# Attention kernel's decay table: lam loaded to one partition and broadcast by matmuls, in place of a broadcast load

## The chip, the cores and the metric

One core of one Trainium2 chip. Times are device microseconds (us) of one execution. A difference of over 2% counts as faster or slower. Every ratio here is of executions in the fast state, with a granted TensorE clock of 0.997 to 1.0.

## The reference, cut to what matters

A linear attention with a decay per head feeds a two-layer network. The decay `lam` is 8 numbers; the kernel needs powers of it for each position.

```python
Dmask   = np.where(rel >= 0, lam[:, None, None] ** rel[None], 0.0)   # rel = i - j in a block
lam_pow = lam[:, None, None] ** (pos + 1)
kv_state = lam ** block * kv_state + einsum(kb * lam ** (block - 1 - pos), vb)
...
h = x @ w_in; g = smelu(h); out = g @ w_out        # 3072 x 512, 512 x 2048, 2048 x 512
```

## The kernel before: the parts that matter

The powers are tables: exp(position * ln lam). They need ln lam on all 128 partitions, so lam was loaded with a broadcast source: 128 rows of the same 32 bytes.

```python
lam_b = const.tile([128, H], F32)
nc.scalar.dma_start(out=lam_b, in_=lam.partition_broadcast(128))
...                                              # GpSimd: identity, iota, masks
NKB, NUB, NV = 3 if len(PF) < 2 else 0, 3, 4
...
for t in vi[:2] + kbd[:2] + ubd[:1]:
    nc.vector.memset(t, 0.0)
for t in vi[2:]:
    nc.gpsimd.memset(t, 0.0)                     # two memsets of 128 x 1024 bf16
pos = const.tile([128, 2, NCB], F32)
nc.scalar.copy(pos, pos_i)
for t in kbd[2:] + ubd[1:]:
    nc.vector.memset(t, 0.0)
ln_lam = const.tile([128, H], F32)
nc.scalar.activation(out=ln_lam, in_=lam_b, func=AF.Ln)
arg = const.tile([128, 2, NCB, H], F32)
nc.vector.tensor_tensor(arg..., _bc(pos...), _bc(ln_lam...), op=AX.mult)
nc.scalar.activation(out=tab_q..., in_=arg[:, 1], func=AF.Exp)      # then tab_p, tab_k
...
def cast(c, eng):          # ks = k * table, on VectorE or GpSimd
    eng.tensor_tensor(ks[c], qkv_ld[c, 1], _bc(tab, 2, D), op=AX.mult)
def cast_q(m, e, eng):     # qs = q * table, on VectorE or GpSimd
    eng.tensor_tensor(qs[m, e], qkv_ld[m, 0][:, :, e], _bc(tab_q..., 2, D), op=AX.mult)
def f_m(c, g):             # sc = scores (PSUM) * causal mask, on VectorE
    nc.vector.tensor_tensor(sc_sb[c][:, g], pst[c, g], _bc(causal, 1, HP), op=AX.mult)
def f_g(...):              # the activation: t, then w, then gT, bf16 in SBUF, on VectorE
```

All instructions are put in an order by a plan at build time; the loads of q, k and v go out on one queue (SP), the weights on GpSimd's. In the profile x0f is q, raw and x1f are k, x2f is v; qs and ks are the products; pt and py are PSUM tiles of the transposes that follow.

## Time and profile before

| | before |
|---|---|
| median of the first 6 runs | 220.57 us (219.85 to 220.69) |
| span of the profiled run | 219.9 us; that run took 221.62 us, 1 us above the median |
| TensorE busy | 203.2 us |
| lam landed, tables ready (tab_q) | 6.30, 7.10 us |
| q, raw k landed | 7.2, 9.0 us |
| first transpose on TensorE | 8.92 us |

The lines behind this stand in the prediction, which was made when three of the six runs were known (median 220.63). The way to read it: a head in which TensorE has nothing to do, then a body in which it is busy.

### The profile page before, as it was taken

The page shows a single profiled execution, that of the slowest core. Times are in us where ns is not written, and L with a number is a line of the kernel's source. Part 1 is how long each engine was busy: PE and PEld are TensorE (multiplying, and loading weights), DVE is VectorE, ACT ScalarE, POOL GpSimd, SP SyncE. Part 2 cuts the span into 40 slices and gives each one's busy share as a digit, 9 for nine tenths or more (in the row PEclk, how much of TensorE's full clock was granted, in tenths as well). Part 3 has the DMA queues.
Part 4 walks back from the last instruction along what each step waited for, and adds up shares of the span by engine and source line. Part 5 has one row for each costly group of instructions (what it writes and reads, how often), then busy time and mean ns, then how long its engine had stood idle before and what let it go on. Part 6 is the DMA issues. An engine that isn't in the chain of part 4 may idle for free.

```text
span 219.9 us, 4453 instructions
## 1 busy us (share of the span) xinstructions
PE 203.2 (92%) x1776; PEld 132.5 (60%) x1800; DVE 139.4 (63%) x216; ACT 123.0 (56%) x220; POOL 63.0 (29%) x71
## 2 busy tenths in 40 slices
PE   0299899999999999999999999999999999999994
PEld 0267778685847977777767676744545444444443
DVE  6285678779553798977855967740697655554301
ACT  2247678455737757486747667545765535445030
POOL 8563085208515162804412700432100000000000
PEclk9999999999999999999999999999999999999999
DMA  3999999999998998989999727989785211110122
GB/s 90 282 218 211 177 244 209 186 205 239 159 224 151 226 184 199 187 162 236 204 244 203 152 43 152 201 196 217 250 141 172 50 45 51 48 48 0 51 95 95
DMA packets 96116, 35.42 MB, mean 161 GB/s; under 512 B 78560, under 2 KB 93152, under 8 KB 96096
## 3 DMA queue, kind: packets, MB, share of 16 engines
q1 hardware_dynamic: 91728, 30.94, 65.6%
q0 software_dynamic: 4224, 4.19, 11.9%
q8 instruction: 14, 0.23, 0.5%
q14 instruction: 6, 0.05, 0.1%
q10 hardware_dynamic: 144, 0.00, 0.0%
HBM read 27.27 MB, written 6.29 MB: 153 GB/s over the span
## 4 chain that ended last, share of the span: by engine, by line
PE 88%; DVE 3%; DMA 2%; ACT 2%; issue 2%; POOL 1%
PE ph L470 38%; PE py L518 35%; DMA lam_b<-in_lam_dram 2%; PE ps L398 2%; PE po L428 2%; PE pu L369 2%; PE py L512 1%; DVE sc L410 1%; PE py L332 1%; PE pt L325 1%; PE po L420 1%; PE po L425 1%; PE pu L365 1%; PE po L446 1%; ACT xT L458 1%
## 5 line engine op out<-in xcount | busy, mean ns | idle before, releaser
L470 PE MATMUL ph<-xT,w_in_sb 128*128 128x256 bf16 (+2 forms) x763 | 95.7, 272 | 1.7 <-ACT xT L458 1.2
L479 ACT ACTIVATE r<-ph,one 128x512 bf16<-128x512 f32 x96 | 65.9, 688 | 48.7 <-PE ph L470 32.0
L518 PE MATMUL py<-w_out_sb,gT 128*128 128x512 bf16 x349 | 86.5, 379 | 1.2 <-issue 0.3
L470 PEld LDWEIGHTS <-w_in_sb 128*128 128x128 bf16 x768 | 63.3, 98 | 24.8 <-issue 1.9
L518 PEld LDWEIGHTS <-gT 128*128 128x128 bf16 x368 | 34.8, 98 | 34.8
L489 DVE TENSOR_SCALAR t<-r 128x1024 bf16<-128x1024 bf16 x48 | 25.1, 524 | 37.0 <-ACT r L479 36.9
L500 DVE TENSOR_TENSOR gT<-w,t 128x1024 bf16<-128x1024 bf16 x48 | 39.6, 826 | 1.5
L495 DVE TENSOR_TENSOR w<-r,t 128x1024 bf16<-128x1024 bf16 x48 | 36.7, 765 | 1.5
L287 POOL TENSOR_TENSOR ks<-x1f,tab_k 128x512 bf16<-128x512 f32 x20 | 23.9, 1199 | 31.4 <-DMA x1f<-in_k_dram 16.5
L523 ACT COPY osb<-py 128x512 f32<-128x512 f32 x23 | 13.5, 586 | 17.9 <-PE py L518 16.6
L296 POOL TENSOR_TENSOR qs<-x0f,tab_q 128x512 bf16<-128x512 f32 x15 | 17.5, 1184 | 19.1 <-DMA x0f<-in_q_dram 12.1
L373 ACT CAST ubd<-pu 64x256 bf16<-64x256 f32 x40 | 14.6, 365 | 6.8 <-PE pu L369 3.7
L294 POOL TENSOR_TENSOR qs<-x0f,tab_qn 128x512 bf16<-128x512 f32 x8 | 9.1, 1134 | 27.7 <-DMA x0f<-in_q_dram 18.7
L410 DVE TENSOR_TENSOR sc<-ps,causal 128x512 bf16<-128x512 f32 x12 | 8.3, 689 | 9.8 <-PE pt L398 9.7
L458 ACT CAST xT<-po 128x512 bf16<-128x512 f32 x15 | 8.8, 585 | 8.2 <-PE po L428 5.0
L332 PE MATMUL py<-ident,qs 128*128 128x128 bf16 x16 | 2.4, 306 | 9.6 <-POOL qs L296 8.9
L428 PE MATMUL po<-sc,vi 128*128 128x128 bf16 x112 | 10.5, 219 | 0.0
L428 PEld LDWEIGHTS <-vi 128*128 128x128 bf16 x112 | 8.4, 98 | 1.0
L410 DVE TENSOR_TENSOR sc<-ps,causal_n 128x512 bf16<-128x512 f32 x8 | 5.5, 689 | 5.2 <-PE pt L398 5.2
L425 PE MATMUL po<-qT,ubd 128*128 128x128 bf16 x48 | 8.7, 219 | 0.0
L320 ACT CAST vi<-x2f 128x512 bf16<-128x512 f32 x14 | 8.5, 615 | 0.1
L332 PEld LDWEIGHTS <-qs 128*128 128x128 bf16 x24 | 2.1, 121 | 10.5 <-POOL qs L296 8.9
(84 smaller groups left out, 137.4 us busy)
## 6 DMA issues: line engine op xcount, KB each, us to landing
out_dram<-osb SPq DMA_DIRECT2D x23, 256.0 KB, 2.7
x1f<-in_k_dram SPq DMA_DIRECT2D x22, 256.0 KB, 4.8
x2f<-in_v_dram SPq DMA_DIRECT2D x22, 256.0 KB, 4.8
x0f<-in_q_dram SPq DMA_DIRECT2D x8, 512.0 KB, 5.3
w_in_sb<-in_moe_w_in_dram POOLq DMA_DIRECT2D x4, 512.0 KB, 8.2
w_out_sb<-in_moe_w_out_dram POOLq DMA_DIRECT2D x4, 512.0 KB, 8.5
x0f<-in_q_dram SPq DMA_DIRECT2D x8, 256.0 KB, 4.1
raw<-in_k_dram SPq DMA_DIRECT2D x1, 512.0 KB, 7.7
```

Of the source, the lines that this page charges most:

```text
L287: eng.tensor_tensor(ks[c], qkv_ld[c, 1], _bc(tab, 2, D), op=AX.mult)
L296: eng.tensor_tensor(qs[m, e], qkv_ld[m, 0][:, :, e], _bc(tab_q[:, e, m % (NCB // 2), :], 2, D), op=AX.mult)
L373: nc.scalar.copy(out=ubd[c % NUB][HD[hi], :, HD[hi]], in_=pu[0][HD[hi], :, HD[hi]])
L410: nc.vector.tensor_tensor(sc_sb[c][:, g], pst[c, g], _bc(causal if c < DX else causal_n, 1, HP), op=AX.mult)
L428: nc.tensor.matmul(po[:, hp], lhsT=vi[c % NV][:, hp, hi].rearrange("p a d -> p (a d)"), rhs=sc_sb[c][:, hi, hp, :], start=(cb == 0 and hi ...
L470: nc.tensor.matmul(ph[:, j * m:(j + 1) * m], lhsT=w_in_sb[:, ko, (ni + j) * 128:(ni + j + 1) * 128], rhs=xT[s][:, ko, tok], start=(ko == 0 ...
L479: nc.scalar.activation(out=o, in_=x, func=AF.Relu, bias=one[:, 0:1])
L489: nc.vector.tensor_scalar(t, r, 0.5, 1.0, op0=AX.mult, op1=AX.min)
L495: nc.vector.tensor_tensor(w, r, t, op=AX.subtract)
L500: nc.vector.tensor_tensor(gT[s][:, f - RW * n:f, tok].rearrange("p (a b) m -> p a b m", a=RW), w.rearrange("p a (b m) -> p a b m", m=m), t ...
L518: nc.tensor.matmul(py_t[s, ms], lhsT=gT[s][:, ko, ms * 128:(ms + 1) * 128], rhs=w_out_sb[:, ko, :], start=(ko == 0), stop=(ko == FO - 1))
L523: nc.scalar.copy(out=osb[s, ms], in_=py_t[s, ms])
```

## The change

The intent: load lam as one small row, so that it lands early; make the logarithm there; spread it to 128 partitions with a matmul against a row of ones. A bf16 matmul would round the logarithm, so it is split into three bf16 pieces that add up to it. One buffer less is set to zero, and a constant of the plan is smaller.

```diff
-    lam_b = const.tile([128, H], F32)
-    nc.scalar.dma_start(out=lam_b, in_=lam.partition_broadcast(128))
+    lam_r = const.tile([1, H], F32)
+    nc.scalar.dma_start(out=lam_r, in_=lam.rearrange("(o h) -> o h", o=1))
...
-    NKB, NUB, NV = 3 if len(PF) < 2 else 0, 3, 4
+    NKB, NUB, NV = 2, 3, 4
...
+    ones = const.tile([1, 128], BF16)
+    nc.vector.memset(ones, 1.0)
-    for t in vi[:2] + kbd[:2] + ubd[:1]:
+    for t in vi[:2] + kbd + ubd:
         nc.vector.memset(t, 0.0)
...
-    for t in kbd[2:] + ubd[1:]:
-        nc.vector.memset(t, 0.0)
-    ln_lam = const.tile([128, H], F32)
-    nc.scalar.activation(out=ln_lam, in_=lam_b, func=AF.Ln)
+    rest = const.tile([1, 3, H], F32)
+    nc.scalar.activation(out=rest[:, 0], in_=lam_r, func=AF.Ln)
+    piece = const.tile([1, 3, H], BF16)
+    for i in range(3):
+        nc.vector.tensor_copy(piece[:, i], rest[:, i])
+        if i < 2:
+            nc.vector.tensor_tensor(rest[:, i + 1], rest[:, i], piece[:, i], op=AX.subtract)
+    ln_ps = pp_s.tile([128, HP, 128], F32, name="ps", tag="ps")
+    ln_lam = ln_ps[:, 0, :H]
+    for i in range(3):
+        nc.tensor.matmul(ln_lam, lhsT=ones, rhs=piece[:, i], start=(i == 0), stop=(i == 2))
...
-    FIRST_BYTE = 2950
+    FIRST_BYTE = 2450
```

## The prediction

> **What bounds the kernel now.** I read the page first: the shares of the engines and the span in slices.
>
> ```profile
> span 219.9 us, 4453 instructions
> PE 203.2 (92%) x1776; PEld 132.5 (60%) x1800; DVE 139.4 (63%) x216; ACT 123.0 (56%) x220; POOL 63.0 (29%) x71
> ...
> PE   0299899999999999999999999999999999999994
> ```
>
> TensorE is busy for 203.2 of 219.9 us, and the 16.7 us in which it isn't lie almost wholly at the two ends. The view of busy time in stretches (columns: stretch, its length, then busy us and instructions of PE, weight loads, DVE, ACT, POOL; granted clock, DMA share, GB/s) says where:
>
> ```profile
> 0.00:9.00 9.00, 0.08 (x1) 0.08 (x2) 4.25 (x11) 2.19 (x6) 6.04 (x18) 1.00 0.69 175
> 9.00:21.00 12.00, 10.44 (x129) 8.21 (x130) 6.90 (x14) 7.08 (x15) 7.02 (x7) 1.00 1.17 218
> 21.00:40.00 19.00, 17.55 (x175) 14.84 (x176) 14.33 (x20) 13.93 (x26) 8.48 (x10) 1.00 1.15 206
> 40.00:60.00 20.00, 19.74 (x230) 14.56 (x232) 15.63 (x23) 11.18 (x19) 8.41 (x8) 1.00 1.04 197
> ```
>
> TensorE idles for 8.92 us before its first instruction, 1.56 us between 9 and 21 us, 1.45 us between 21 and 40 us, and from 40 us on about 0.2 us in each 20 us. So the kernel is a head of 8.92 us followed by a TensorE-bound body, with 3.2 us of tail after 216 us. Whatever shortens the head should arrive at the end nearly whole, as long as the body keeps its work and its order. Then I read the chain that ended last, in order of time, for 0 to 9 us (start, duration, what):
>
> ```profile
> 0.83 5.47 DMA lam_b<-in_lam_dram
> 6.30 0.02 issue
> 6.32 0.22 ACT ln_lam L144
> 6.54 0.02 issue
> 6.57 0.27 DVE arg L146
> 6.84 0.02 issue
> 6.86 0.24 ACT tab_q L149
> 7.10 0.13 ACT tab_p L151
> 7.23 0.09 issue
> 7.32 1.56 POOL qs L296
> 8.88 0.05 issue
> 8.92 0.29 PE py L332
> ```
>
> The load of the 8 numbers of lam takes 5.47 us, and three table steps (ln_lam, arg, tab_q) take 0.8 us after it. It looks as if all of this could go. It can't: the product qs also needs q. The list of DMA issues, cut to the one issue at 0.81 us, gives its time to landing:
>
> ```profile
> x0f<-in_q_dram SPq DMA_DIRECT2D x1, 512.0 KB, 6.4
> ```
>
> So q lands at 0.81 + 6.4 = 7.2 us, 0.1 us after tab_q is ready (6.86 + 0.24 = 7.10) and level with tab_p. The chain names the tables, but q is level with them. **This is the main fact of the case**: faster tables by themselves win some 0.1 us. The gain is what q, and k after it, land earlier.
>
> Does removing the wide lam load make q earlier? The DMA view for 3 to 4 us and for 6 to 7 us (q10 carries lam, q1 the loads):
>
> ```profile
> DMA packets 250, 0.10 MB, mean 97 GB/s; under 512 B 65, under 2 KB 250, under 8 KB 250
> q10 hardware_dynamic: 65, 0.00, 3.2%
> ```
>
> ```profile
> DMA packets 684, 0.35 MB, mean 345 GB/s; under 512 B 10, under 2 KB 684, under 8 KB 684
> ```
>
> By stretches of 1 us from 2 us on the rates are 133, 97, 134, 284 and 345 GB/s, and q10 has 3, 65, 49, 27 and no packets. The rate is lowest where lam's packets are densest, and it is full as soon as they are over. That is a coincidence in time, not yet a cause.
>
> **What the Trainium skill says.** "DMA: Bandwidth & Descriptors", section "Queues, rings and completion order": each of the 16 DMA engines takes turns between the queues for which it has work. Lam's packets lie among q's from 3 to 6 us in this trace, which agrees. Same page, "Why a DMA increments its semaphore by 16 and not by 1": a transfer has landed when the last of its engines has posted. The profile page counts 144 packets on q10, which is 128 rows and 16 posts, so lam waits for the slowest of 16 rings. "VectorE: DVE Perf Modes", section "The TRN2 errata": an fp32 tensor_tensor takes (N+151)/0.96 ns. For N = 96 that is 257 ns; the trace has 0.26 us for arg. "TensorE: Matmul & The Clock Gate", section "Single matmul latency": (398+N)/2.4 ns. For N = 128 that is 219 ns; the trace has 219 ns for L428.
>
> **The change part by part.**
>
> 1. Lam to one partition. It removes 127 of 128 row packets and at least 8 of the 16 posts. Its issue stays at 0.83 us. In the trace lam's first packets come at about 3 us (3 of them in 2 to 3 us), since they come behind the first of q's; a transfer with one row, or a few, needs the first of these and a post, so I estimate its landing at 3.4 to 4.2 us, middle 3.8, in place of 6.30.
>
> 2. Set-up on DVE. Before, its memsets run from 0.88 to 4.49 us: 2 of vi in 1.03, 2 of kbd in 1.02, one kbd in 0.48, three ubd in 0.82. One kbd goes (-0.48), a ones row comes (0.06 as for the other small one). DVE is free at about 4.1 us, which is when the logarithm arrives (3.8 + 0.02 + 0.22 = 4.04). Nothing of it is on the path now, as DVE waits 2.08 us for the logarithm. It would be just level with it in the new order.
>
> 3. The splitting. Five dependent DVE operations on 1 x 8 elements: three casts, two subtractions. By the skill's formula a subtraction is (8+151)/0.96 = 166 ns; I take the same for a cast. Between dependent operations of DVE the timeline shows some 0.03 us (t at 24.07 lasts 0.43, w follows at 24.53). Five times 0.166 and four times 0.03 make 0.95 us: 4.1 to 5.05.
>
> 4. Three matmuls of 8 columns with one row. The first two hide under the splitting. The last is (398+8)/2.4 = 169 ns, with two hops of 0.03 us: 0.23 us, to 5.28. Eight columns of TensorE time while it is idle cost nothing.
>
> 5. The tables. arg reads PSUM now: 0.27 to 0.30 us; tab_q 0.24, hops 0.04: ready at about 5.85, tab_p at 5.98. Before: 7.10 and 7.23. So the logarithm costs 1.2 us more than before (0.95 + 0.23), and lam's landing gives 2.5: 1.25 us net.
>
> 6. q. It is 1024 packets of 512 B. By the same view q1 had moved 11 packets by 2 us, and then 260, 185, 263 and 563 in the next four stretches of 1 us, so the 1024th went at about 5.5 us, and q's landing at 7.2 lags that by 1.65 us (the slowest engine, and the receipt). Without the dip I let the fourth and fifth us have 260 to 350 and 350 to 560 packets: the 1024th then goes at about 4.7 to 5.2, and q lands at 6.3 to 6.9. The diff has an opinion of its own: the first-byte constant of the scheduling plan goes from 2950 to 2450 ns, so its writer saw or guessed loads that come 0.5 us earlier: 6.7. I take 6.45. So q, not the tables, ends the head: qs starts at about 6.52 in place of 7.32, 0.8 us earlier.
>
> 7. k and v. The next products wait for them too: DVE's ks waited 1.11 us, to 9.07, for raw k (1.32 + 7.7 = 9.02). The transposes that need it run at 10.58, after ks ends at 9.76: 0.8 us of slack. They come off the same queue as q, so they should move by about as much as q.
>
> The sum: 0.8 us off the head, all of which I count at the end but for 0.07 us, since TensorE is busy for over 98% from 40 us on. 220.63 - 0.73 = **219.9 us**, 0.3%. Even if the whole of lam's wait were won, from 6.30 to 3.8, it would be 2.5 us or 1.1%: the change cannot reach 2% by its mechanism.
>
> **Rivals.** (a) *q is bound by something other than lam*: packets of the first load come slowly for their own reason (descriptors of the first transfers being made), and lam's are only spread by that. For it: before lam's first packet, in 2 to 3 us, the rate is only 133 GB/s, and lam's own packets fill 3.2% of the engines' time. Then q lands at 7.1 to 7.2, nothing is won but the 0.1 us: 220.4 to 220.7. (b) *The lam load was the whole brake*: q lands at 5.3 to 5.8, the tables become the bound at 5.98, qs starts at 6.1: 1.2 us, 219.4; with k and v earlier also some of the 1.56 us of idle time between 9 and 21 us, 218.9. (c) *The plan changes order*: the new constant moves the plan's landing times, and the list order of every engine follows from them. A small inversion in the head (a cast before a table, a transpose before its product) costs or wins 0.3 to 1 us; over the body TensorE's idle time of 0.2 us in 20 us leaves little to win, but a worse order could lose some 1 to 2 us. 218.6 to 221.5. (d) *The one-row chain is much slower than counted*, by 0.3 us per small step: tables at 7.5, slower by 0.3 us: 220.9.
>
> **Range and chances.** I give (a) 0.25, my sum 0.4, (b) 0.25, (d) 0.1, and let (c) widen each by about 0.6 us to both sides; repeats of the kernel before span 0.67 us. The range is 218.7 to 220.9. Faster by over 2% needs 216.2, which no rival reaches but a lucky order: 0.02. Slower by over 2% needs 225.0, an order that breaks the body: 0.02. Within 2%: 0.96.
>
> **What would show it right or wrong.** q10 with a few packets; lam landing at 3.4 to 4.2; DVE's five small operations between 4.1 and 5.1; tab_q ready at about 5.9; qs released by the load of q and not by a table, at 6.3 to 6.9; raw k landed at 8.1 to 8.6; the first matmul of qs at about 8.1 in place of 8.92; 1 us bins from 3 to 5 us at 200 GB/s or more. Wrong: q landing at 7.2 with the same dip in the rate (then (a)), tables after q (then (d)), or a head shorter by 0.8 us whose gain is lost after 21 us (then (c)).

## The result, and the profile after

Ratios here are the mean time of one kernel's fast runs over that of the other's fast runs of the same rounds, so not quite the ratio of the medians quoted.

| | before | after |
|---|---|---|
| median of 6 runs | 220.57 us | 221.83 us (221.33 to 222.58) |
| ratio, 95% interval | | 1.0066 (1.0041 to 1.0091) |
| span of the profiled run | 219.9 us | 220.9 us (222.58 us, the slowest of the six) |
| lam's packets (q10) | 144 | 2 |
| tab_q ready | 7.10 us | 7.00 us |
| q, raw k landed | 7.2, 9.0 us | 5.1, 6.9 us |
| first transpose | 8.92 us | 8.69 us |

The kernel became slower by 0.66%, within the 2% band but outside the stated range: a miss. The order of the instructions, first. Compared row by row on each engine, the two kernels differ only in the set-up that the diff writes; on SP and GpSimd not one row differs, and a build of the changed kernel with the old constant 2950 gives the same program. So the constant did nothing, and the change of the plan (rival c) is out. All 1800 weight loads of TensorE of before stand in both traces in one order (three more for lam after), so they can be compared one to one.

The loads did more than I had counted. In the changed kernel's page q10 has two packets, in its DMA view from 3 to 4 us the rate is full (before: 97 GB/s), and its list of issues gives q's time to landing:

```profile
q10 hardware_dynamic: 2, 0.00, 0.0%
...
DMA packets 667, 0.34 MB, mean 341 GB/s; under 512 B 1, under 2 KB 667, under 8 KB 667
...
x0f<-in_q_dram SPq DMA_DIRECT2D x1, 512.0 KB, 4.3
```

q lands at 0.81 + 4.3 = 5.1, 2.1 us earlier than before, and k and v with it (raw k 1.33 + 5.6 = 6.9, raw v 1.93 + 6.8 = 8.7, against 9.0 and 10.7). But the tables did not follow. The timeline of the changed kernel's head (start, duration, engine, line, operation; in brackets the idle time before it and what ended it):

```profile
2.21 0.20 ACT L144 ACTIVATE rest<-lam_r 1x8 f32<-1x8 f32 x1
...
3.60 1.83 POOL L140 MEMSET vi<- 128x1024 bf16 x2
4.00 1.46 DVE L147 CAST piece<-rest 1x8 bf16<-1x8 f32 x1
...
5.49 0.15 DVE L149 TENSOR_TENSOR rest<-rest,piece 1x8 f32<-1x8 f32 x1
...
6.28 0.16 PE L153 MATMUL ps<-piece,ones 1*128 1x8 bf16 x1 [0.22 <-DVE piece L147]
6.48 0.25 DVE L155 TENSOR_TENSOR arg<-pos,ps 128x96 f32<-128x96 f32 x1 [0.25 <-PE ps L153]
6.76 0.24 ACT L158 ACTIVATE tab_q<-arg 128x48 f32<-128x48 f32 x1 [4.35 <-DVE arg L155]
...
7.09 1.54 POOL L305 TENSOR_TENSOR qs<-x0f,tab_q 128x512 bf16<-128x512 f32 x1 [1.65 <-ACT tab_q L158]
```

The logarithm was ready at 2.41. VectorE finished its memsets at 4.0, and then the cast of eight numbers took 1.46 us: it ended with GpSimd's pair of memsets (3.60 + 1.83 = 5.43), where the same cast later took 0.16. So tab_q came at 7.00, and qs, now waiting for the table alone, started 0.23 us earlier than before. That is the whole gain of the head; q had lain there for 1.9 us.

Then the body gave back more than that. The start of each weight load after, less that of the same load before: -0.24 us at the first, +0.13 at number 56 (14.4 us in the profile of before), +0.26 at 124 (20.1), +0.73 at 439 (52.4), +1.17 at 1135 (120.0), +0.93 from 1209 (127.1) to the end. The steps are places, not a slope. What leads to the one at 52.4 us, in the kernel before, from the timeline:

```profile
48.56 0.42 DVE L489 TENSOR_SCALAR t<-r 128x1024 bf16<-128x1024 bf16 x1
49.02 0.69 DVE L495 TENSOR_TENSOR w<-r,t 128x1024 bf16<-128x1024 bf16 x1
49.36 2.25 POOL L296 TENSOR_TENSOR qs<-x0f,tab_q 128x512 bf16<-128x512 f32 x2 [8.99 <-DMA x0f<-in_q_dram]
49.73 0.69 DVE L410 TENSOR_TENSOR sc<-ps,causal 128x512 bf16<-128x512 f32 x1
```

and after (the lines of the source stand nine further down):

```profile
48.60 2.67 POOL L296 TENSOR_TENSOR ks<-x1f,tab_k 128x512 bf16<-128x512 f32 x2
49.11 1.26 DVE L498 TENSOR_SCALAR t<-r 128x1024 bf16<-128x1024 bf16 x1
50.41 1.41 DVE L504 TENSOR_TENSOR w<-r,t 128x1024 bf16<-128x1024 bf16 x1
51.74 0.68 DVE L419 TENSOR_TENSOR sc<-ps,causal 128x512 bf16<-128x512 f32 x1
...
53.07 0.22 PE L437 MATMUL po<-sc,vi 128*128 128x128 bf16 x1 [0.26 <-DVE sc L419]
```

GpSimd's qs, released by a load, came at 49.36 before, when t was through and w half done; the stretching then fell on later work (the next gT took 1.22 us), for which TensorE is not seen to wait. After, the same qs came at 46.18 (its load was earlier) and ks at 48.60, so that t took 1.26 in place of 0.42 and w 1.41 in place of 0.69, the mask sc started 2.0 us later, and TensorE waited for it. The place at 14.7 us is of the same kind: VectorE's ks of x1f took 1.27 us at 13.19 beside GpSimd's qs, where it took 0.68 before. I call such a stretch beside GpSimd a collision. The total isn't larger: t, w and gT together took 101.4 us before and 100.6 after. What changed is which instructions it hits.

The page "SBUF — State Buffer" of the Trainium skill, section "Who interferes with whom", states it: a VectorE instruction in a two-port mode (copies and casts can be) contends with GpSimd, one with two SBUF inputs contends with a GpSimd instruction that reads SBUF, and not with one that only writes; the one that comes second waits. I had not used it. The cast of 1.46 us beside a memset, and 0.09 us below for a two-input form of it, agree.

### The profile page after: what moved, and what is told of

It is laid out like the page before. It is cut to its first block, busy times and chain, and to the rows that moved or that the text cites.

```text
span 220.9 us, 4463 instructions
## 1 busy us (share of the span) xinstructions
PE 204.1 (92%) x1779; PEld 133.3 (60%) x1803; DVE 141.3 (64%) x221; ACT 122.8 (56%) x220; POOL 64.5 (29%) x71
## 4 chain that ended last, share of the span: by engine, by line
PE 86%; DVE 6%; POOL 3%; issue 2%; ACT 2%; POOLq 0%; DVEq 0%
PE ph L479 37%; PE py L527 34%; PE po L437 3%; PE ps L407 2%; PE pu L378 2%; DVE w L504 1%; PE py L521 1%; DVE t L498 1%; PE po L434 1%; DVE sc L419 1%; PE py L341 1%; PE pt L334 1%; PE po L429 1%; PE po L455 1%; ACT xT L467 1%
## 5 line engine op out<-in xcount | busy, mean ns | idle before, releaser
L498 DVE TENSOR_SCALAR t<-r 128x1024 bf16<-128x1024 bf16 x48 | 25.8, 537 | 39.0 <-ACT r L488 39.0
L504 DVE TENSOR_TENSOR w<-r,t 128x1024 bf16<-128x1024 bf16 x48 | 38.2, 796 | 1.5
L509 DVE TENSOR_TENSOR gT<-w,t 128x1024 bf16<-128x1024 bf16 x48 | 36.6, 762 | 1.5
L296 POOL TENSOR_TENSOR ks<-x1f,tab_k 128x512 bf16<-128x512 f32 x20 | 24.5, 1229 | 29.8 <-DMA x1f<-in_k_dram 13.6
L305 POOL TENSOR_TENSOR qs<-x0f,tab_q 128x512 bf16<-128x512 f32 x15 | 18.0, 1220 | 18.8 <-DMA x0f<-in_q_dram 11.8
L303 POOL TENSOR_TENSOR qs<-x0f,tab_qn 128x512 bf16<-128x512 f32 x8 | 9.6, 1202 | 30.4 <-DMA x0f<-in_q_dram 25.8
L419 DVE TENSOR_TENSOR sc<-pt,causal 128x512 bf16<-128x512 f32 x12 | 8.1, 679 | 0.0
L407 PE MATMUL pt<-qT,kT 64*128 64x128 bf16 x80 | 7.9, 219 | 0.0
```

The lines of the kernel that those rows point to most:

```text
L498: nc.vector.tensor_scalar(t, r, 0.5, 1.0, op0=AX.mult, op1=AX.min)
L504: nc.vector.tensor_tensor(w, r, t, op=AX.subtract)
L509: nc.vector.tensor_tensor(gT[s][:, f - RW * n:f, tok].rearrange("p (a b) m -> p a b m", a=RW), w.rearrange("p a (b m) -> p a b m", m=m), t ...
```

## The experiments

Two theories of the loss. **Theory 1**: the first cast waits for GpSimd's memset, so the tables stay late while the loads come 2.1 us early; products (qs, ks) that lag their loads shift GpSimd's work against VectorE's, and the collisions fall on masks that TensorE waits for. **Theory 2**: the new chain, or the fewer buffers, cost in themselves; what the loads do is beside the point. A third theory came with the data: each run draws its collisions by chance.

All were correct. Ratios are to the kernel before on the same chip in the same rounds; the median of before was 221.42, 221.18, 222.02 and 221.63 us on the four chips used, with fast runs from 219.66 to 223.56, more spread than in the first six, and slower: the first six averaged 220.39 us, these chips 221.18 to 221.98.

### First chip: the brake, the cast, the early chain

**a_wide**: the old wide load issued as well, behind the narrow one.

```diff
+    lam_b = const.tile([128, H], F32)
+    nc.scalar.dma_start(out=lam_b, in_=lam.partition_broadcast(128))   # nobody reads it
```

> The changed kernel with the old wide load of lam (to all 128 partitions) issued as well, right after the narrow one, into a tile that nobody reads. It tells whether the wide load is what brakes the loads of q, k and v, and whether the earlier loads are what costs time in the body. Theory 1 (earlier loads shift GpSimd's products against VectorE's work, so that they collide elsewhere): q lands again at about 7.2 us (5.1 in the changed kernel), raw k at about 9.0, the first 1 us stretches again at 100 to 135 GB/s; the products start at about 7.3, TensorE runs level with the kernel before all the way, ratio to before 0.998 to 1.002. Theory 2 (the new chain or the fewer buffers cost in themselves): slower than before by 0.4 to 0.8% whatever the loads do. Theory 3 (the loads sped up for another reason than the wide load's absence): q lands at about 5.1 and the ratio stays at 1.0066.

Measured 222.32 us, 1.0026 (0.9988 to 1.0064). The run did not do what I had planned: the wide load, issued 0.6 us later than in the kernel before, came behind q, which landed at 0.81 + 4.2 = 5.0. It braked the next loads instead: raw k at 8.1 in place of 6.9, and 167 and 173 GB/s from 4 to 5 and from 5 to 6 us, where the changed kernel has 311 and 291. So the wide load is a brake; for the times it says little.

**a_tt**: the casts as products of two inputs.

```diff
-        nc.vector.tensor_copy(piece[:, i], rest[:, i])
+        nc.vector.tensor_tensor(piece[:, i], rest[:, i], _bc(one[0:1, 0], 1, H), op=AX.mult)
```

> The changed kernel with its three casts to bf16 written as products with 1 of two inputs, in place of copies; the values are the same. In the changed kernel the first cast, of 1 x 8 elements, took 1.46 us beside GpSimd's memset. Theory 1 (the copy runs in a mode that shares a port with GpSimd, a two-input operation does not wait for a memset): the first cast takes 0.16 us, tab_q is ready at about 5.7 in place of 7.0, the products start at 5.7 (VectorE) and 5.75 (GpSimd), TensorE's first transpose at about 7.4 in place of 8.69. The loads stay 2.1 us earlier than before, so products and loads are again nearly in the relation of the kernel before: I expect 0.994 to 0.999 of before. Theory 2 (a first operation on one partition, or on a fresh ScalarE result, is slow): the cast takes 1.4 us again and the time stays at 1.006.

Measured 220.31 us, 0.9936 (0.9896 to 0.9977). From the timeline of its head:

```profile
3.60 1.83 POOL L140 MEMSET vi<- 128x1024 bf16 x2
4.00 0.09 DVE L147 TENSOR_TENSOR piece<-rest,one 1x8 bf16<-1x8 f32 x1
...
5.39 0.24 ACT L158 ACTIVATE tab_q<-arg 128x48 f32<-128x48 f32 x1 [2.99 <-DVE arg L155]
```

The same place and memset, 0.09 us in place of 1.46: the wait of the cast is shown. The tables, ready at 5.64, still came after q (5.10). TensorE started 1.61 us ahead of before and lost most of it: -1.44 at weight load 430, -0.98 at 438, -0.44 one load later, again at the place at 52 us. This profile is of the slowest of the six runs.

**a_early** and **a_f32**: the chain ahead of most memsets. In a_early the casts go to ScalarE; in a_f32 there is no splitting.

```diff
# a_early
-    for t in vi[:2] + kbd + ubd:
+    for t in vi[:2]:
         nc.vector.memset(t, 0.0)
-    for t in vi[2:]:
-        nc.gpsimd.memset(t, 0.0)
...
-        nc.vector.tensor_copy(piece[:, i], rest[:, i])
+        nc.scalar.copy(piece[:, i], rest[:, i])
...                                              # after arg:
+    for t in kbd + ubd + vi[2:3]:
+        nc.vector.memset(t, 0.0)
+    nc.gpsimd.memset(vi[3], 0.0)
# a_f32: likewise, with ones and rest in F32, no pieces, kbd[0] set before arg, and
+    nc.tensor.matmul(ln_lam, lhsT=ones, rhs=rest, start=True, stop=True)
```

> The changed kernel with the chain of lam ahead of most memsets of VectorE, the casts on ScalarE, and one of the two memsets of GpSimd moved to VectorE. Theory 1: tab_q is ready at 4.3 to 5.0 us, before q lands at 5.1; the products start at about 5.2 on both engines, 2.1 us earlier than before, by as much as the loads are earlier, so the relation of loads and products is that of the kernel before and no new collisions come: TensorE starts at about 6.8 and stays 1.8 to 2.1 us ahead to the end, ratio 0.990 to 0.992. Rival (the body loses by early loads as such, or by chance collisions of any shift): ahead by 2 us at the start and by less than 1 at the end, ratio 0.996 or more.

> As the kernel with the early chain, but with no splitting at all: one matmul of fp32 operands in place of three of bf16, no casts and no subtractions. Theory 1: tab_q ready at about 3.6 us, q at 5.1 binds alone, products at about 5.15, ratio 0.990 to 0.992, the same as the early chain within 0.1%, which says that the chain is off the path there. Correct to the same error if fp32 operands are carried exactly enough; if it is not, the error is larger than that of the kernel before.

Measured 218.96 us, 0.988 (0.9843 to 0.9917), and 219.37 us, 0.9887 (0.9848 to 0.9927). The chain of waits of a_f32:

```profile
0.81 4.21 DMA x0f<-in_q_dram
...
5.17 1.56 POOL qs L300
```

Here q alone ends the head, as I had predicted for the changed kernel. TensorE runs 2.15 us ahead of before at its first weights and 2.22 at the end: where products and loads move together, the body takes nothing back. These are the best versions: 1.1 to 1.2% below before, a little more than the 0.8 to 1.0% expected.

### Second chip: loads moved, tables left alone

**after_again** is the changed kernel. **a_brake** and **f32_brake** put a useless load in front of q's, in the changed kernel and in a_f32:

```diff
+    scratch = const.tile([128, H, 2, D], F32)
+    nc.sync.dma_start(out=scratch.rearrange("p h e d -> p h (e d)"),
+                      in_=q[B - 1, :, S - 2 * C:, :].rearrange("h (j e) d -> j h (e d)", e=2))
     run_plan(...)
```

> The changed kernel once more, beside the next ones on the same chip. All theories: 1.004 to 1.009 of before, TensorE 0.24 us ahead at its first weights, 0.9 to 1.2 us behind at the end.

> The changed kernel with a useless load of 512 KB, of the same form as the first load of q, put ahead of it on the same queue. It moves all loads some 1.5 to 1.7 us later, back to near the times of the kernel before, while the tables stay ready at 7.0 us, and the order of all engines is the same. Theory 1 (the body loses by the relation in time of loads and GpSimd products to VectorE's work): q lands at about 6.8, still ahead of the tables, so the head is as in the changed kernel, but the relation is again that of the kernel before; TensorE keeps its 0.24 us to the end, ratio 0.997 to 1.001, faster than the changed kernel by 0.5 to 0.9% with half a megabyte more to load. Theory 2 (the new chain costs in itself): 1.005 to 1.009, as without the brake. Theory 3 (early loads crowd the DMA queues): between the two.

> The same useless load in front of the kernel with the early fp32 chain, whose head is bound by q alone (q at 5.1, tables at 3.6 without the brake). Theory 1: products and loads move together, so nothing but the head changes: TensorE starts 1.5 to 1.7 us later than without the brake and stays so to the end, some 0.4 us ahead of before: ratio 0.996 to 1.000, slower than without the brake by 0.7 to 0.8%. With the run before this crosses: the same load makes one kernel faster and the other slower. Rival: both become slower by it.

| | median | ratio to before | 95% interval |
|---|---|---|---|
| after_again | 221.78 us | 1.0034 | 0.9999 to 1.0069 |
| a_brake | 221.31 us | 1.0007 | 0.9976 to 1.0038 |
| f32_brake | 220.90 us | 0.9993 | 0.9964 to 1.0022 |

The head of a_brake is that of the changed kernel (tab_q at 7.0, first transpose at 8.69), but VectorE waited for raw k until 8.82, as before it did until 9.07. after_again itself came out below the 1.004 that every theory had as its least. Half a megabyte more to load made the changed kernel 0.27% faster, half of the least that I expected and not clear of noise by itself, and it made a_f32 1.1% slower (0.9887 without it, on another chip). The crossing is there. In a_brake's timeline the place at 50 us looks as before (GpSimd's pair of qs starts at 48.59, when t is through):

```profile
47.77 0.42 DVE L498 TENSOR_SCALAR t<-r 128x1024 bf16<-128x1024 bf16 x1
48.23 0.69 DVE L504 TENSOR_TENSOR w<-r,t 128x1024 bf16<-128x1024 bf16 x1
48.95 0.69 DVE L419 TENSOR_TENSOR sc<-ps,causal 128x512 bf16<-128x512 f32 x1
```

**w_same**: the wide load again, ahead of the narrow one (the two lines of a_wide, put before the load of lam_r).

> The changed kernel with the old wide load of lam issued as well, this time ahead of the narrow one, so that it stands where it stood in the kernel before (in the earlier run it was issued behind, came 1.3 us later, let q through at 5.0 and braked k and what follows by 1.2 us). If the wide load is the brake: q lands at 6.8 to 7.3, the stretch from 3 to 4 us falls to about 100 GB/s, all loads are again where they were before. The narrow load then may land later than 2.2; if it lands by 4 the tables are ready at 7.0 as in the changed kernel and theory 1 gives 0.997 to 1.002; if it lands at 6 the tables come at about 8, and the kernel is slower than before by 0.4 to 0.6%. If the wide load is not the brake: q at 5.1 and 1.0066.

Measured 221.77 us, 1.0021 (0.9988 to 1.0054). q landed at 0.81 + 5.6 = 6.4, in place of 5.1, and the stretch from 3 to 4 us fell to 131 GB/s. So it is a brake, of 1.3 us here, where all of the difference of before and after was 2.1. The narrow load, behind it, let ScalarE start only at 5.13; the cast then came after GpSimd's memsets, took 0.16 us, and tab_q was ready at 7.07. Loads and products were near the relation of neither kernel (raw k 0.6 us ahead of the first transpose), so this run does not decide between the theories.

### Third chip: late tables without the chain, and what brakes

**f32_late**: a_f32 with arg behind all of VectorE's memsets and four useless ones.

```diff
     for t in kbd[1:] + ubd + vi[2:3]:
         nc.vector.memset(t, 0.0)
+    for _ in range(4):
+        nc.vector.memset(kbd[1], 0.0)
     arg = ...                                   # was ahead of these memsets
```

> The kernel with the early fp32 chain (1.1% faster than before), with its product arg put behind all memsets of VectorE and four useless ones of 0.5 us more, so that the tables are ready at about 7.0 us as in the changed kernel. It has no splitting, no casts and no collision of a cast; the loads stay 2.1 us early. Theory 1 (late products on early loads make the collisions of the body): TensorE starts at about 8.7, 0.2 us ahead of before, raw k lands 1.8 us ahead of the first transpose, and the body from the first to the last weights is 0.5 to 1.2 us longer than that of the kernel before, as in the changed kernel; ratio 1.002 to 1.007. Theory 2 (the splitting and its matmuls cost in the body): ratio 0.997 to 1.000, as nothing of them is in it.

Measured 222.0 us, 0.9995 (0.9955 to 1.0035). The tables came at 7.5, later than planned, and the first transpose at 9.20. The ratio lies where theory 2 had it and below what theory 1 had, though theory 1's 1.002 to 1.0035 is in the interval. Its profile shows a step of 0.47 us at weight load 439, the place of the changed kernel, with no splitting in it, but elsewhere the body gained. It did not decide, and it made me doubt: hence the fourth chip.

**w_dist** and **w_512**: one look each. The wide load ahead of lam's with 128 different addresses, of 32 and of 512 bytes.

```diff
+    lam_b = const.tile([128, H], F32)
+    nc.scalar.dma_start(out=lam_b, in_=q[0, 0, 0:128, 0:H])
# w_512: [128, 2 * D], in_=q[0, 0, 0:256, :] with 512 bytes to a row
```

> The changed kernel with a useless wide load of 128 x 32 bytes ahead of lam's, as in the run where the old wide load stood first (q then landed at 6.4 in place of 5.0), but from 128 different addresses 256 bytes apart in q, where lam's wide load reads the same 32 bytes 128 times. If many reads of one address are the brake: q lands at 5.0 to 5.3 and the stretch from 3 to 4 us keeps over 300 GB/s. If it is the number of packets or of small ones: q at 6.2 to 6.6, and 100 to 150 GB/s in that stretch.

> The same with 128 packets of 512 bytes in place of 32. If a second queue by itself slows the first one: q at 6.2 or later. If small packets do, or the one address: q at 5.0 to 5.4, later only by the 64 KB more, some 0.2 us.

Run times 221.50 and 222.21 us (one run each). The DMA view from 3 to 4 us of w_same (128 times one address), then of w_dist (128 addresses):

```profile
DMA packets 320, 0.13 MB, mean 131 GB/s; under 512 B 67, under 2 KB 320, under 8 KB 320
```

```profile
DMA packets 642, 0.33 MB, mean 326 GB/s; under 512 B 5, under 2 KB 642, under 8 KB 642
...
lam_b<-in_q_dram ACTq DMA_DIRECT2D x1, 4.0 KB, 1.7
```

With different addresses the wide load landed in 1.7 us (3.8 for lam's in w_same, 5.5 in the kernel before), q at 0.81 + 4.1 = 4.9, as if it were not there; with 512 bytes to a row q landed at 5.1. So it is not the number of packets, nor their size, nor a second queue: what is left is that 128 rows read the same 32 bytes. These are one profile each, and their useless load reads q and not lam, so that something peculiar to lam's place in memory is not ruled out.

### Fourth chip: is it a lottery?

**before_again**, **after_third**, **a_brake_2**, **a_f32_2**: the kernels of those names once more, side by side.

> The kernel before itself, as one of the kernels tried, for a second profile of it and for the noise: on two of the chips its runs spread over 2.8 us and more. Ratio 0.997 to 1.003. If the body's losses are collisions that depend on run-to-run timing, its second profile shows the first weights at the same 9.2 us and an end that differs from that of the first by up to 1 us, with stretched VectorE operations at the places where the time differs.

> The changed kernel on one chip with the kernel before, the braked one and the early one. Theory 1 (late products on early loads collide more): 1.003 to 1.007. Lottery (each chip and run draws its collisions, whatever the relation): anything from 0.996 to 1.006.

> The changed kernel with the useless 512 KB load ahead of q, again. Theory 1: below the changed kernel of the same rounds by 0.3 to 0.8%, 0.996 to 1.001 of before. Lottery: level with the changed kernel within 0.2%.

> The kernel with the early fp32 chain, again, as the best of the versions on the same chip: 0.987 to 0.991 by both.

| | median | ratio to before | 95% interval |
|---|---|---|---|
| before_again | 221.78 us | 1.0025 | 0.9988 to 1.0062 |
| after_third | 222.07 us | 1.0030 | 0.9999 to 1.0060 |
| a_brake_2 | 221.25 us | 1.0010 | 0.9971 to 1.0050 |
| a_f32_2 | 218.98 us | 0.9892 | 0.9861 to 0.9923 |

The same code of before, built again, came out at 1.0025, so a quarter of a per cent is noise here, and the changed kernel's 0.3% on two chips is not far from it. The brake made the changed kernel faster again, by 0.49 us of mean (222.05 against 221.56), after 0.60 us on the second chip (221.85 against 221.25). By itself the 0.2% lies between the two expectations. Taken together, 12 runs against 12, that is 0.55 us with a standard error of 0.22.

The profiles can leave the head out. The time from TensorE's eleventh weight load of the program proper to its last, by trace:

| raw k against the first transpose | kernels | body, us | mean |
|---|---|---|---|
| lands with it or after it | before 205.81, before_again 205.94, a_brake 205.03, a_brake_2 205.66, f32_brake 205.04, a_f32 205.75, a_f32_2 205.14, a_early 205.52 | 205.03 to 205.94 | 205.49 |
| landed 0.4 us or more ahead | after 206.99, after_again 206.36, after_third 206.08, a_tt 206.99, a_wide 206.88, w_same 206.36, w_512 206.65, w_dist 205.92, f32_late 205.86 | 205.86 to 206.99 | 206.45 |

The step at weight load 439 (the lag behind the first profile of before at load 445, less that at 430) is 0.42 us or more in six of the nine of the second row (after, after_again, a_tt, a_wide, w_512, f32_late), and at most 0.18 in the eight of the first. The line between the rows was drawn after the runs (a_tt, w_same and a_wide lie at 0.4 to 0.6 us), the rows overlap a little, and each kernel stands by one profiled execution: that of a_brake was the fastest of its six, those of a_tt and after the slowest. Shifting each body by the difference between the mean of the six runs and the profiled run gives an estimate of 205.5 and 206.3 us for the rows, 0.8 us apart (0.6 without before, whose profiled run lay 1.2 us above its six; w_dist and w_512 have one run and are left out).

So both are at work: each run draws its collisions, within about 1 us, and early loads under late products move the draw by some 0.6 to 1 us. Theory 2 falls: a_early and a_f32 keep the fewer buffers, a_brake keeps the whole chain with them, and their bodies are no longer than those of before. (a_tt can't speak here: its body is as long as that of after.) What I have not shown is each single collision's part, as none was taken away alone, nor why before spread more on the later chips.

## Why the prediction was wrong, point by point

Two steps failed: the first cast of the splitting, counted at 0.166 us, took 1.46, so that the tables came at 7.00 in place of 5.85; and the head's gain was counted to the end, where the body gave it back and more.

- *The bound, head and body.* Right: TensorE has no slack after the head. It was read in one direction only. A body without slack also passes on every new delay, and the step "all of which I count at the end but for 0.07 us" failed: TensorE began 0.24 us earlier, not 0.8, and the body of the changed kernel took 0.3 to 1.2 us longer in its three profiles than in the first of before. Besides these, 16.7 us of idle time "almost wholly at the two ends" is loose: head and tail are some 12 us of it.
- *Lam's landing* (3.4 to 4.2): earlier still; the logarithm began at 2.21. Off the path, as VectorE was busy to 4.0.
- *DVE free at 4.1*: 4.00, right.
- *The splitting, 0.95 us*: the term that failed first. Four of the five operations took 0.15 to 0.16 us, as worked out; the first cast took 1.46 in place of 0.166, beside GpSimd's memset. That memset stood in the timeline of before at 3.62 to 5.45, and the casts were put into just that stretch; I never asked what runs beside them.
- *Matmuls and tables*: 0.16 us and 0.25 us, right. tab_q came at 7.00 in place of 5.85, nearly all by the cast.
- *q, 6.45*: 5.1. The cause was the right one (lam's load brakes q), but the size was that of half a brake: 667 packets went from 3 to 4 us, where I had let 260 to 350, and by the same count the landing lagged the 1024th packet by 0.9 us, where I had kept 1.65. The constant of the plan pulled me to the late side. I had left open whether it was packets or something else; w_dist and w_512 leave the one address.
- *"So q, not the tables, ends the head"*: wrong, for both reasons together. With only the cast's wait removed the tables (5.64) still end the head (a_tt); with the chain put ahead of the memsets q does (a_early, a_f32).
- *Rivals.* (b), the whole brake, was nearest: q at 5.3 to 5.8 (5.1 in fact), the tables as the bound at 5.98 and 218.9 to 219.4 us. a_tt is that kernel (tables at 5.64), and 0.9936 of 220.57 is 219.2; the agreement is partly luck, as its head won 1.6 us and its body gave some back. (c) looked for the change of order in the plan; there was none. Its 1 to 2 us lost in the body came near (0.3 to 1.2 in the profiles) by luck, for another cause: the same order at other times. (d) was the right place, tables held up by the small chain, by one step of 1.3 us.
- *The chances* (within 2%) held; the range did not, by 0.9 us. The size of the loss, 0.66%, is in part the luck of the first six runs of before: on two later chips it was 0.3%, which is not clear of noise. That the forecast gain did not come holds on all three.

## What to carry to other kernels

When a change makes data arrive earlier, ask what the engine that waited for it will now run beside, and look first at VectorE and GpSimd, which hold each other up. Move loads and the work that uses them together: here both 2 us earlier gave 1.1%, and the loads almost alone gave nothing. And do not broadcast a few bytes from memory to all partitions beside loads that matter; load one row and spread it on the chip.

## What the Trainium skill lacked or had wrong

- "DMA: Bandwidth & Descriptors" has nothing on many reads of one address: 128 rows that read the same 32 bytes held the other queue to 131 GB/s for a microsecond and made q 1.3 us later (2.1 between before and after); 128 different addresses cost nothing that the one profile shows (326 GB/s, landing in 1.7 us in place of 3.8).
- "SBUF — State Buffer", section "Who interferes with whom", says that the second one waits for the whole instruction of the first, and nothing of two in a row. Here a cast that started at 4.00 waited for two GpSimd memsets in a row, of 0.94 us each, and ended at 5.46, not soon after the end of the first at 4.54.
- "VectorE: DVE Perf Modes" checked its formula for an fp32 tensor_tensor at 512 and 2048 elements; at 8 it works out to an estimate of 166 ns, and on one partition the subtractions took 0.15 us.
- "TensorE: Matmul & The Clock Gate" has no time for an fp32 matmul: one of 8 columns and one row stands in the trace as two weight loads and two matmuls, 0.59 us from the first weights to the end, where one of bf16, its weights loaded before, took 0.16.
